# Hashed attention with adapters: a new order in the first head pair, adapter weight loads moved, and a finer split of weighted values

## The chip, the cores and the metric

The kernel runs on 1 core of one Trainium2 chip. The metric is the device time of one execution in microseconds (us), here the median of 5 executions. One more execution was recorded by the hardware profiler; it gives the profile page and the trace.

The engines have short names: PE is TensorE (matrix multiply; PEld is its weight load), ACT is ScalarE, DVE is VectorE, POOL is GpSimd, SP is SyncE, which only issues transfers.

## The reference, cut to what matters

Attention over 4 x 8 heads of 768 rows with 64 features. Each query and key gets a hash of 6 sign bits, and a query sees only the keys with its own hash. Then comes a mixture of 8 adapters of rank 16, two of them chosen per row.

```python
q_bits = (einsum('bhsd,dk->bhsk', q, proj) > 0)        # k_bits likewise, 6 bits
mask = q_bucket[:, :, :, None] == k_bucket[:, :, None, :]
scores = where(mask, (q @ k.T) / sqrt(D), -1e9)
attn = softmax(scores); x = attn @ v                    # x: [3072, 512]
logits = x @ w_gate; top two of 8, softmax over the two
out = x + sum over the two of w * ((x @ A[e]) @ B[e])
```

## The kernel before, in words

The 32 heads are worked in 16 pairs, p = 0 to 15. For a pair, queries and keys are transposed on PE (`trans`, line 232: three groups of four 128x128 transposes, each copied out of PSUM at line 249 by DVE or at line 247 by ACT into `qkT`). `hash` (line 256) multiplies `qkT` with the projection (line 262) and DVE turns the result into +-0.5 (`sgn`, line 265). Four small DMAs on SP (`sign_dma`, line 167; two from `hash`, two from `hash_b`) carry these rows into partitions 64 to 69 of the tile `aug`, which has the features in partitions 0 to 63 (`cast`, line 276, on POOL). Scores are taken over 71 rows of `aug`, so that the hash decides inside the same matmul.

The scores of a pair are made in 9 tiles of 128x1024 (`score`, line 320), one in each slot s = 0 to 8: two or three matmuls at line 327, then one exponential on ACT at line 329. There are two score buffers, so the matmuls of a tile wait for the exponential two tiles before. `pvmm(p, h, i0, i1)` (line 338) multiplies the exponentials of head h with the values `vb`, six matmuls at line 334 for each of six row groups i. `uniform` (line 358) makes a small term for rows without a match, `norm` (line 368) adds it on DVE, divides and writes `x`; after the second head POOL casts `x` into `xb`. `vcast` (line 218) prepares the values on POOL.

The order of work on every engine is written out by hand: the loop in `run` calls, in each slot, `score`, then `first_pair` (p = 0) or `pair` (p = 1 to 14) and `moe_slot`; `last_pair` does the last one. Each engine takes its instructions in that order, and what one needs from another is a wait on a semaphore. Pair p prepares pair p + 1 (last transposes in slot 0, casts in slot 1, hash in slot 2) and starts the transposes of pair p + 2 in slots 5 and 7. PSUM has eight banks: two score buffers of two banks each (`ps_s`), one bank T (`ps_t`), two banks V (`ps_v`) and one bank M (`ps_m`). Transposes and hashes go to T unless another bank is named.

In the first pair the kernel has nothing prepared. The prologue brings pair 0 far enough for its first score tiles; the hashes of the second head of pair 0 (`signs1`, line 155) and everything of pair 1 are done between the score tiles of pair 0, in `first_pair` (line 606).

The adapter weights are loaded on POOL's DMA queue by `load_moe(i)` (line 171): i = 0 the gate, 1 to 4 one slice of `A` each, 5 `B`. Gate and `A` go into the tile `wa`, first read in pair 5; `B` goes into `Bcat`, first read in slot 6 of pair 5. The adapters of a batch of four pairs are computed in the pairs of the next one, in groups of row slots given by `moe_group`: one or two slots for the first batches, three for batch 2 (pairs 13 and 14). `moe_slot` (line 571) does this: logits in slots 0 and 1 (line 480), the choice of experts (lines 489 to 513), a transpose in slot 4 (line 534), and `delta` from slot 6 on (line 548 on PE, line 556 on DVE).

Of the kernel before, what the change touches and what calls it, by code (L numbers as in the profile page):

```python
# [19 lines left out]
class Emitter:  # L20
# [585 lines left out]
    def first_pair(self, s):  # L606
        T, M, V = (self.ps_t, "t"), (self.ps_m, "m"), (self.ps_v, "v")
        if s == 0:
            self.load_qk(2)
            self.load_v(1)  # L610
            self.load_v(2)
        if s == 1:
            self.signs1(3, (T, M))
            self.trans(1, 0, bank=V)
        if s == 2:
            self.signs1(2, (T, M))
        if s == 3:
            self.trans(1, 1, on_act=True, bank=V)
            self.trans(1, 2)
            self.cast(1, 0)  # L620
            self.cast(1, 1)
        if s == 4:
            self.hash(1)
            self.hash_b(1)
        if s == 5:
            self.trans(2, 0, bank=M)
            self.vcast(1)
            self.load(3)
        if s == 6:
            self.pvmm(0, 0, 0, 2)  # L630
            self.uniform(0)
        if s == 7:
            self.pvmm(0, 0, 2, 4)
            self.trans(2, 1, bank=M)
        if s == 8:
            self.pvmm(0, 0, 4, 6)
            self.load_moe(0)
            self.load_moe(1)

    def pair(self, p, s):  # L640
        n = len(self.moe_group(p)[1])

        for at, i0, i1 in ((1, 0, 1), (3, 1, 3), (4, 3, 5), (5, 5, 6)) if n == 2 else ((1, 0, 2), (3, 2, 4), (4, 4, 6)):
            if s == at:
                self.pvmm(p - 1, 1, i0, i1)
        if s == 0:
            self.norm(p - 1, 0)
            self.trans(p + 1, 2)
            self.load_qk(p + 3, (0,))
        if s == 1:  # L650
            self.cast(p + 1, 0)
            self.cast(p + 1, 1)
        if s == 2:
            self.hash(p + 1)
            if p + 1 == self.n_pairs - 1:
                self.hash_b(p + 1)
            self.load_qk(p + 3, (1,))
        if s == 4:
            self.uniform(p)
            if p + 1 < self.n_pairs - 1:  # L660
                self.hash_b(p + 1)
        if s == 5:
            self.norm(p - 1, 1)
            self.vcast(p + 1)
            self.trans(p + 2, 0, on_act=n > 1)
            if p < 4:
                self.load_moe(p + 1)
            if p == 3:
                self.load_moe(5)
        if s == 6:  # L670
            self.pvmm(p, 0, 0, 2)
        if s == 7:
            if p % self.PPB:
                self.xturn(p - 1)
            self.trans(p + 2, 1)
            self.pvmm(p, 0, 2, 3)
        if s == 8:
            self.pvmm(p, 0, 3, 6)
            if p % self.PPB == 0:
                self.xtrans(p - 1, bank=(self.ps_m, "m"))  # L680
            self.load_v(p + 3)

    def last_pair(self, p, b):
        t = [(0, 1), (2, 3), (4, 5)]
# [101 lines left out]
```

## Time and profile before

| | us |
|---|---|
| median of 5 executions | 174.6 (173.92 to 175.15) |
| the profiled execution's own time | 174.27 |
| its span, first to last instruction | 172.5 |
| mean granted PE clock | 0.982 |
| score matmuls, line 327, x408 | 86.1 busy |
| value matmuls, line 334, x1080 | 48.1 busy |
| transposes, line 242, x180 | 27.9 busy |
| copies out of PSUM, line 249, x39 | 26.7 busy, 685 ns each |
| casts, line 280, x30 | 43.9 busy, 1463 ns each |

Matmuls overlap, so their busy time is longer than the time they hold the queue; the distance from one start to the next is the better measure. The exponentials follow each other at 0.90 to 0.92 us where nothing holds them up. The first exponential of a pair begins at these times, so that the distance is a pair's length:

| pair | first exponential, us | length, us |
|---|---|---|
| 0 | 8.54 | 10.69 |
| 1 | 19.23 | 9.22 |
| 2 | 28.45 | 8.86 |
| 3 | 37.31 | 8.86 |
| 13 | 130.70 | 10.61 |
| 14 | 141.31 | 9.87 |
| 15 | 151.18 | |

DMA issues on SP from the end of pair 0 are in this order: four sign transfers of pair 1 (15.43 to 18.86), the loads of pair 3 and half of those of pair 4 (18.96 to 20.88), two sign transfers of pair 2 (22.33), and so on. The transfers of the gate and of the first piece of `A` are issued on POOL at 19.86 and 20.77.

### The profile page before, as it was taken

To read this page: it belongs to the slowest core of one execution; us is meant where nothing else is said; L and a number is where in the kernel's file an instruction comes from. 1 tells how busy PE (TensorE), PEld (TensorE's weight loads), DVE (VectorE), ACT (ScalarE), POOL (GpSimd) and SP (SyncE) were. 2 spreads that over 40 slices of the span, in tenths; PEclk is the share of its full clock that TensorE was granted. 3 is DMA by queue.
4 is the path that set the end of the run, shared out by engine and by line. 5 is a ranking of instruction groups with operands and counts; after the bars stand their busy time and mean duration, and the time that the engine had idled before them with its cause. 6 is when DMAs were issued, how large, how long until landed. Compare 5 with 4: busy or idle time off the path is not lost.

```text
span 172.5 us, 5262 instructions
## 1 busy us (share of the span) xinstructions
PE 162.0 (94%) x2109; PEld 112.1 (65%) x2109; DVE 117.6 (68%) x315; ACT 151.1 (88%) x177; POOL 115.5 (67%) x140
## 2 busy tenths in 40 slices
PE   7999999999999999999999999999999999998850
PEld 5445667676757576767667676767687766687600
DVE  4865666564746787778687787868785776647770
ACT  3688998999998999999998999999998988997750
POOL 8289989597988657576756677686766566630280
PEclk9999999999999999999999999999999999999975
DMA  5990399769997139577876258586944024240036
GB/s 171 283 351 22 121 264 226 122 146 187 131 237 244 43 117 281 159 183 262 122 263 189 77 150 301 130 242 209 230 137 151 10 48 184 57 184 4 2 144 222
DMA packets 30402, 28.49 MB, mean 165 GB/s; under 512 B 15066, under 2 KB 28458, under 8 KB 30378
## 3 DMA queue, kind: packets, MB, share of 16 engines
q1 hardware_dynamic: 24984, 27.36, 54.6%
q0 software_dynamic: 4832, 0.27, 4.7%
q10 hardware_dynamic: 562, 0.53, 0.9%
q8 instruction: 16, 0.26, 0.6%
q14 instruction: 8, 0.07, 0.1%
HBM read 19.42 MB, written 6.29 MB: 149 GB/s over the span
## 4 chain that ended last, share of the span: by engine, by line
PE 78%; DVE 8%; DMA 4%; POOL 3%; issue 2%; ACT 1%; SPq 1%; DVEq 0%; ACTq 0%; POOLq 0%
PE s L327 31%; PE pv L334 16%; PE tr L242 12%; PE hs L262 7%; PE lz L480 3%; DMA aug<-sgn 3%; PE dl L548 2%; PE hsd L146 2%; DMA nat<-in_k_dram 2%; DVE qkT L249 2%; PE xtp L463 1%; DVE acc L556 1%; PE trf L125 1%; DVE x L384 1%; POOL xb L390 1%
## 5 line engine op out<-in xcount | busy, mean ns | idle before, releaser
L329 ACT ACTIVATE P<-s 128x1024 bf16<-128x1024 f32 x144 | 139.7, 1028 | 9.1 <-PE s L327 7.5
L327 PE MATMUL s<-aug 71*128 71x256 bf16 (+2 forms) x408 | 86.1, 316 | 0.6 <-ACT P L329 0.3
L334 PEld LDWEIGHTS <-P 128*128 128x128 bf16 x1080 | 45.4, 98 | 11.8
L280 POOL CAST aug<-qkT 64x1536 bf16<-64x1536 f32 x30 | 43.9, 1463 | 11.9 <-DVE qkT L249 9.6
L334 PE MATMUL pv<-vb,P 128*128 128x65 bf16 x1080 | 48.1, 193 | 0.0
L327 PEld LDWEIGHTS <-aug 71*128 71x128 bf16 x408 | 32.6, 97 | 19.1 <-issue 11.1
L249 DVE TENSOR_SCALAR qkT<-tr 128x512 f32<-128x512 f32 x39 | 26.7, 685 | 7.9 <-PE tr L242 6.0
L390 POOL CAST xb<-x 128x768 bf16<-128x768 f32 x15 | 12.3, 822 | 25.3 <-DVE x L384 23.2
L242 PE MATMUL tr<-ident,nat 128*128 128x128 f32 x180 | 27.9, 278 | 0.0
L242 PEld LDWEIGHTS tr<-ident,nat 128*128 128x128 f32 x180 | 20.3, 140 | 7.5 <-DVE qkT L249 3.1
L265 DVE TENSOR_SCALAR sgn<-hs 128x384 bf16<-128x384 f32 x15 | 8.4, 557 | 13.3 <-PE hs L262 11.9
L384 DVE TENSOR_TENSOR x<-pv,ri 128x384 f32<-128x384 f32 x30 | 16.7, 557 | 1.0
L556 DVE SCALAR_TENSOR_TENSOR acc<-dl,rt,x 128x512 f32<-128x512 f32 (+1 forms) x21 | 14.9, 719 | 3.3 <-PE dl L548 3.3
L379 DVE TENSOR_TENSOR pv<-pv,uni 128x390 f32<-128x390 f32 x24 | 13.6, 568 | 3.4 <-PE pv L334 3.3
L225 POOL TENSOR_TENSOR vs<-vn 128x384 f32<-128x384 f32 x16 | 15.9, 993 | 0.0
L262 PE MATMUL hs<-qkT,proj 128*32 128x384 f32 x120 | 12.8, 498 | 0.6 <-DVE qkT L249 0.3
L223 POOL CAST vb<-vn 128x768 bf16<-128x768 f32 x16 | 13.2, 825 | 0.1
L554 POOL TENSOR_TENSOR acc<-tmp,x 128x512 f32<-128x512 f32 x4 | 5.0, 1264 | 8.8 <-ACT tmp L553 8.8
L548 PE MATMUL dl<-Bcat,zmT 128*128 128x512 bf16 x24 | 9.5, 397 | 0.9 <-ACT zmT L537 0.8
L480 PE MATMUL lz<-wa,xT 128*128 128x136 bf16 x96 | 9.3, 223 | 0.6 <-ACT xT L465 0.6
L366 DVE COPY uni<-un 128x130 f32<-128x130 f32 x12 | 3.5, 294 | 6.8 <-PE un L364 6.8
L228 POOL TENSOR_TENSOR vb<-vs,vs 128x128 bf16<-128x128 f32 x16 | 7.3, 458 | 1.3
(70 smaller groups left out, 126.0 us busy)
## 6 DMA issues: line engine op xcount, KB each, us to landing
vn<-in_v_dram SPq DMA_DIRECT2D x16, 384.0 KB
nat<-in_q_dram SPq DMA_DIRECT2D x15, 384.0 KB
nat<-in_k_dram SPq DMA_DIRECT2D x15, 384.0 KB
out_dram<-acc SPq DMA_DIRECT2D x4, 512.0 KB
out_dram<-acc SPq DMA_DIRECT2D x8, 256.0 KB
out_dram<-acc SPq DMA_DIRECT2D x2, 768.0 KB
aug<-sgn SPq DMA_DIRECT2D x60, 9.0 KB
nat<-in_q_dram SPq DMA_DIRECT2D x2, 192.0 KB
```

The lines of the kernel that those rows point to most:

```text
L225: nc.gpsimd.tensor_add(out=s3, in0=vn[:, :, 0:3, :], in1=vn[:, :, 3:6, :])
L242: nc.tensor.transpose(out=ps[:, j * P:(j + 1) * P], in_=self.nat[p][:, idx % 2, idx // 2, u * P:(u + 1) * P], identity=self.ident)
L249: nc.vector.tensor_scalar(out=out, in0=ps, scalar1=2.0 ** -5, scalar2=None, op0=ALU.mult)
L262: nc.tensor.matmul(out=ps[32 * j:32 * j + 32, :], lhsT=self.proj2, rhs=self.qkT[p][:, j * 384:(j + 1) * 384], start=True, stop=True)
L280: self.nc.gpsimd.tensor_copy(out=self.aug[p % 2][0:64, :, e * n:(e + 1) * n], in_=self.qkT[p][64 * e:64 * e + 64, :].rearrange("p (j c) -> ...
L327: nc.tensor.matmul(out=ps[:, o:o + n], lhsT=aug[0:71, 2 * h + 1, kt * P:(kt + 1) * P], rhs=q, start=True, stop=True)
L329: nc.scalar.activation(out=self.P_[p][:, s * 1024:(s + 1) * 1024], in_=ps, func=ACT.Exp, scale=128.0)
L334: self.nc.tensor.matmul(out=pv, lhsT=self.p_at(p, h, kt, i), rhs=self.vb[p % 3][:, h, self.slot(kt), :], start=(start and kt == 0), stop=( ...
L384: nc.vector.tensor_tensor(out=self.x[b][:, :, c:c + D].rearrange("p (u e) d -> p e u d", e=2), in0=pv[:, 0:T, 0:D].rearrange("p (e u) d -> ...
L390: nc.gpsimd.tensor_copy(out=self.xb[b][:, hp], in_=self.x[b][:, :, hp * P:(hp + 1) * P])
L480: nc.tensor.matmul(out=lz[:, i, :], lhsT=self.xT[b][:, t, s * P:(s + 1) * P], rhs=self.wa[:, t, :], start=(t == 0), stop=(t == self.nD - 1))
L556: nc.vector.scalar_tensor_tensor(out=acc[:, i, c], in0=ps[:, c], scalar=self.rt[b, slots][:, i:i + 1], in1=self.x[b][:, slots[i], c], op0= ...
```

## The change

In the first pair the transposes of pair 1 begin one slot later and use other banks, and the second hash of slot 2 uses both V banks. The hash of pair 1 moves from slot 4 to slot 5, behind the sixth score tile, with its sign transfers and, behind them, the loads of pair 3. The first two transposes of pair 2 move from slots 5 and 7 to slots 7 and 8, and `uniform` uses bank M. The gate load moves from pair 0, slot 8, to pair 2, slot 8, and the load of `B` from pair 3, slot 5, to pair 4, slot 2. The values of the second head, which pairs with two adapter slots split over slots 1, 3, 4 and 5 as 1 + 2 + 2 + 1 row groups, are now split so with three adapter slots too (pairs 13 and 14), where they were 2 + 2 + 2 over slots 1, 3 and 4.

```diff
--- before.py
+++ after.py
@@ -611,36 +611,34 @@
             self.load_v(2)
         if s == 1:
             self.signs1(3, (T, M))
-            self.trans(1, 0, bank=V)
         if s == 2:
-            self.signs1(2, (T, M))
+            self.signs1(2, (V, V))
+            self.trans(1, 0)
         if s == 3:
-            self.trans(1, 1, on_act=True, bank=V)
-            self.trans(1, 2)
+            self.trans(1, 1, on_act=True, bank=M)
+            self.trans(1, 2, bank=V)
             self.cast(1, 0)
             self.cast(1, 1)
-        if s == 4:
+        if s == 5:
             self.hash(1)
             self.hash_b(1)
-        if s == 5:
-            self.trans(2, 0, bank=M)
+            self.load(3)
             self.vcast(1)
-            self.load(3)
         if s == 6:
             self.pvmm(0, 0, 0, 2)
-            self.uniform(0)
+            self.uniform(0, bank=M)
         if s == 7:
             self.pvmm(0, 0, 2, 4)
-            self.trans(2, 1, bank=M)
+            self.trans(2, 0)
         if s == 8:
             self.pvmm(0, 0, 4, 6)
-            self.load_moe(0)
+            self.trans(2, 1, bank=M)
             self.load_moe(1)
 
     def pair(self, p, s):
         n = len(self.moe_group(p)[1])
 
-        for at, i0, i1 in ((1, 0, 1), (3, 1, 3), (4, 3, 5), (5, 5, 6)) if n == 2 else ((1, 0, 2), (3, 2, 4), (4, 4, 6)):
+        for at, i0, i1 in ((1, 0, 1), (3, 1, 3), (4, 3, 5), (5, 5, 6)) if n > 1 else ((1, 0, 2), (3, 2, 4), (4, 4, 6)):
             if s == at:
                 self.pvmm(p - 1, 1, i0, i1)
         if s == 0:
@@ -655,6 +653,8 @@
             if p + 1 == self.n_pairs - 1:
                 self.hash_b(p + 1)
             self.load_qk(p + 3, (1,))
+            if p == self.PPB:
+                self.load_moe(5)
         if s == 4:
             self.uniform(p)
             if p + 1 < self.n_pairs - 1:
@@ -665,8 +665,6 @@
             self.trans(p + 2, 0, on_act=n > 1)
             if p < 4:
                 self.load_moe(p + 1)
-            if p == 3:
-                self.load_moe(5)
         if s == 6:
             self.pvmm(p, 0, 0, 2)
         if s == 7:
@@ -679,6 +677,8 @@
             if p % self.PPB == 0:
                 self.xtrans(p - 1, bank=(self.ps_m, "m"))
             self.load_v(p + 3)
+            if p == 2:
+                self.load_moe(0)
 
     def last_pair(self, p, b):
         t = [(0, 1), (2, 3), (4, 5)]
```

In the order of the instructions, the number of instructions of each engine is the same in both kernels.

## The prediction

> **What bounds the kernel now.** I write (p, s) for score tile s (0 to 8) of pair p. The page comes first: two engines are nearly full, and the exponentials alone fill 139.7 us, 1028 ns each.
>
> ```profile
> PE 162.0 (94%) x2109; PEld 112.1 (65%) x2109; DVE 117.6 (68%) x315; ACT 151.1 (88%) x177; POOL 115.5 (67%) x140
> q0 software_dynamic: 4832, 0.27, 4.7%
> L329 ACT ACTIVATE P<-s 128x1024 bf16<-128x1024 f32 x144 | 139.7, 1028 | 9.1 <-PE s L327 7.5
> ```
>
> ScalarE is idle only 9.1 us before exponentials, 7.5 of them for TensorE. So a microsecond is won only where both the exponentials and TensorE's queue come forward. The second line is the adapter weights: tiny packets, but 4.7% of 16 engines. Next, the chain of waits from 7 to 38 us (start, length, what):
>
> ```profile
> 13.13 0.70 DVE qkT L249
> 13.87 0.85 PE hs L262 x8
> 14.72 0.54 PE s L327 x3
> ...
> 20.34 0.55 PE s L327 x3
> 20.89 0.83 PE hs L262 x8
> 21.74 0.57 DVE sgn L265
> 22.33 0.75 SPq L168
> ...
> 23.13 4.53 DMA aug<-sgn
> 27.66 0.09 issue
> 27.75 0.59 PE s L327 x3
> ```
>
> Two things are to be seen. In pair 0 the hash of pair 1 stops TensorE's queue at 13.87 until VectorE has copied the transposes. At the end of pair 1, tile (2,0) starts at 27.75, right after the sign rows of pair 2 landed at 27.66, 4.53 us after the issue. The timeline puts the 18 weighted-value matmuls before it at 26.84 to 27.36 (start of the last), so TensorE was free at about 27.42: 0.33 us lost. The view of stretches shows why that landing was late (pair 1, pair 2; the last two figures are DMA share and GB/s):
>
> ```profile
> 18.49:27.75 9.26, 9.06 (x122) 6.07 (x119) 5.53 (x13) 8.98 (x10) 8.49 (x10) 1.00 1.02 229
> 27.75:36.70 8.95, 8.95 (x118) 6.10 (x119) 5.13 (x11) 8.29 (x10) 6.99 (x9) 1.00 0.83 161
> ```
>
> In pair 1 the DMA engines are full. Then the timeline of VectorE around the step from pair 0 to pair 1:
>
> ```profile
> 17.87 0.69 DVE L249 TENSOR_SCALAR qkT<-tr 128x512 f32<-128x512 f32 x1 [0.98 <-PE tr L242]
> ...
> 18.67 0.57 DVE L379 TENSOR_TENSOR pv<-pv,uni 128x390 f32<-128x390 f32 x1
> ...
> 19.51 0.56 DVE L384 TENSOR_TENSOR x<-pv,ri 128x384 f32<-128x384 f32 x1
> ...
> 19.98 0.68 DVE L249 TENSOR_SCALAR qkT<-tr 128x512 f32<-128x512 f32 x1
> ```
>
> It ends at 20.66, and the hash of pair 2 starts at 20.82. Last, TensorE in pair 14:
>
> ```profile
> 145.42 0.60 PE L327 MATMUL s<-aug 71*128 71x512 bf16 x2
> 145.86 0.53 PE L334 MATMUL pv<-vb,P 128*128 128x65 bf16 x12
> 146.35 0.34 PE L534 MATMUL ztp<-ident_bf,zm 128*128 128x128 bf16 x3
> 146.53 1.31 PE L327 MATMUL s<-aug 71*128 71x256 bf16 x6
> ```
>
> Twelve value matmuls take 0.37 us of queue, six take 0.19.
>
> **What the Trainium skill says.** "TensorE: Matmul & The Clock Gate", Part 3, The mechanism: matmuls are "strict FIFO, no reordering". The trace agrees: (0,5) needs nothing from the hash, and starts only behind it, at 14.66. "PSUM — Partial Sum Buffer", Engine vs sequencer instructions: ScalarE, VectorE and GpSimdE queues are strict FIFO; a copy put ahead of the norm delays the norm. "DMA: Bandwidth & Descriptors", Issuing engines are not separate DMA queues: whatever engine issues them, transfers share the same 16 engines and interleave; the 1.02 above agrees. The same page, Specifications, wants 512 B or more per transfer for line rate: here 4832 small packets took 4.7% x 172.5 x 16 / 4832 = 27 ns each.
>
> **Part 1, the first pair.** Nothing is added or removed; order and PSUM banks change. I replay it with the measured starts.
> - (0,2) now stands directly behind the hash of slot 1 (second pass at 9.20, next matmul 0.41 later) instead of behind four transposes (9.61 to 10.10). It waits for exponential 0 (8.54 + 1.02 = 9.57): about 9.65 for 10.10. Its exponential is then bound by ScalarE, 9.46 + 0.92 = 10.38 for 10.74.
> - The hash of slot 2 uses the two V banks, free since 8.82. It and then the transposes run behind (0,2): 1.25 us to the first transpose (0.22 + 0.30 + 0.32 + 0.41, the starts seen before), 0.49 to (0,3): 11.39 for 11.60. Eight transposes as before (0.45 + 0.87): (0,4) at 12.71 for 12.92, its exponential at 13.44 for 13.65.
> - (0,5) now has no hash in front: 13.15 for 14.66. Its exponential follows at 13.44 + 0.92 = 14.36 for 15.30. Here the first pair is 0.94 us ahead.
> - The hash of pair 1 waits for the copy of the last transposes: PE end 12.88, copy 12.94 to 13.63, hash 13.68 for 13.87. So although it stands one tile later, it runs 0.19 us earlier. Exponentials 6 and 7 follow at 15.27 and 16.17 (before 16.22, 17.12). GpSimd gains nothing: its two casts start behind line 114 at 14.02 as before.
> - The sign rows come 0.19 us earlier. Completion marks in the trace put the second of them at 18.40 now, against the start of (1,0) at 18.49. TensorE would be ready for (1,0) at 17.97, and waits until about 18.30. No bulk load lies in front of these rows on SP, whose order keeps the signs ahead of the loads.
> - The transposes of pair 2 move from slots 5 and 7 to 7 and 8. The second group is now at 17.54 (0,8 at 16.72, values 17.16), behind the values instead of before tile 8 at 17.20. Its copy starts at 18.21 for 17.87. VectorE goes in order: add 18.81, reciprocal 19.42, x 19.65, last copy 20.12 to 20.81. So the hash of pair 2 starts at 20.86, before 20.82.
>
> So the 0.94 us of lead is first cut to 0.2-0.3 by the sign rows and then to nothing (-0.04) by VectorE. This is the step that I trust least: at best, with the lead kept whole, 0.95 is won; at worst 0.2 us is lost.
>
> **Part 2, the adapter weights.** The gate weights (512 runs of 8 numbers: 128 partitions x 4) leave pair 0's slot 8 for pair 2's. At 27 ns they cost 512 x 27 / 16 = 0.86 us of all engines, an estimate; one A piece with 1024 runs costs 1.7. In pair 1 the rows of pair 2 wait behind four loads and both adapter pieces. Without the gate, and with loads issued 0.19 earlier, they land about 0.9 us earlier, near 26.7, before TensorE's 27.46. The 0.33 us wait goes, minus the 0.04: 0.29 won. If only a third of that relief comes, half of the gain remains. GpSimd's issue (0.91 us) goes from 19.86 as well; its casts then end at 23.75 for 24.66, needed only at 27.46, so worth nothing. In pair 2's slot 8 the gate goes in front of the casts of pair 4 (38.91 to 41.91 now) and pushes them to about 42.8. Behind them stands xb at 43.29, which waits 1.38 us for VectorE and covers it. The transfer may delay the sign rows of pair 4, which landed at 43.22; (4,0) needs them at about 45.5, so 0.86 fits. If the cover is gone, as in pair 1, at most 0.3 us is lost. The move of Bcat (0.56 us of GpSimd) from pair 3 to pair 4 is covered in the same way: xb at 52.16 has 0.84 us of idle before it, and Bcat is needed at pair 5's slot 6.
>
> **Part 3, pairs 13 and 14 (three adapter slots).** Six value matmuls move from slot 1 to 3, six from 3 to 4, six from 4 to 5. Everything between comes 0.19 us earlier. In pair 13 this is given back: slot 5's transposes start where they did, 136.23, and tile 8 and the wait of the last delta for VectorE (140.40) stay. In pair 14 no transposes follow. Tiles 2 to 5 start 0.19 earlier (146.34 for 146.53), tile 6 waits for exponential 4, itself earlier (147.06 for 147.25), and the deltas follow. The norm comes 0.19 later on VectorE (x 147.42 for 147.23) but ends at 147.97, just as the delta needs VectorE. Worth 0.19 us, between 0 and 0.25. The cast of the last values on GpSimd ends at 151.73 for 151.54, needed at 152.9.
>
> **Sum.** 0.29 + 0.19 = 0.48 us. After pair 2 all stages are relative to TensorE's queue, so it is carried to the end. The profiled execution took 174.27 us (span 172.5): 173.79. The median is 174.6: **174.1 us**.
>
> **Rivals.**
> - Lead kept (B): the wait at the sign rows and VectorE's chain are shorter than I reckon, as ScalarE is 0.95 us ahead at tile 7. 0.95 + 0.33 + 0.19 = 1.47 us: 173.1. For it: the lead up to tile 7 is plain. Against: rows at 18.2, and strict order on VectorE.
> - Rows late anyway (C): the wait at 27.66 comes from the loads, not from the gate weights. Then 0.15 to 0.2 us: 174.4.
> - Slower (D): the hash now stands behind (0,5), and if its rows take 4.53 us, as in pair 1, instead of about 2, the second lands at 16.31 + 4.53 = 20.84 and (1,0) starts at 20.93. The hash of pair 2 then follows 2.15 us later, 23.08 for 20.82: 2.3 us lost, 0.5 won back, 176.4. It decides from a landing past 19.1. Against: no load is under way from 14.5 to 19.
> - The change does what it says in all three parts, by the order of instructions; that is no rival.
>
> **Numbers.** A 50%, B 25%, C 12%, D 13%. This kernel can tell about 0.5%, 0.87 us, from no change. Faster: B nearly whole and a quarter of A, where small terms add up (0.24 + 0.13). Slower: D. The rest is the same. Range 173.0 to 175.0: it takes in B and C and leaves out D and B's lower edge.
>
> **What would show it.** Right: (0,5) at about 13.2; (1,0) at 18.2-18.4 beside the landing; the hash of pair 2 at 20.8-20.9; no DMA wait before (2,0); pair 14 shorter by 0.19 and pair 13 not. Wrong: a hash of pair 2 at 20.0 (B), a chain that still holds 4 us of sign rows in pair 1 (C), (1,0) past 19.1 (D).

## The result and the profile after

| | before | after |
|---|---|---|
| median, us | 174.43 (45 executions, 173.67 to 175.4) | 173.74 (26 executions, 173.26 to 174.64) |
| profiled execution, its span | 174.27, 172.5 | 173.32, 171.5 |

The ratio after to before is 0.9962, with a 95% interval of 0.9947 to 0.9976: 0.66 us won, with 0.42 to 0.92 us possible. The prediction said 0.48 us and 174.1 us.

The head of the page of after, in the order engines, adapter queue, chain by engine, exponentials:

```profile
PE 161.3 (94%) x2109; PEld 112.0 (65%) x2109; DVE 117.7 (69%) x315; ACT 151.2 (88%) x177; POOL 115.6 (67%) x140
...
q0 software_dynamic: 4832, 0.27, 4.9%
...
PE 82%; DVE 9%; POOL 3%; issue 2%; ACT 0%; DVEq 0%; ACTq 0%; POOLq 0%
...
L329 ACT ACTIVATE P<-s 128x1024 bf16<-128x1024 f32 x144 | 139.6, 1028 | 8.7 <-PE s L327 7.0
```

No engine does less work: the busy times are those of before within 0.7 us. What is gone is waiting. ScalarE's idle time for TensorE is 7.0 us (7.5 before), and no DMA stands in the third line any more. On the page of before that line was

```profile
PE 78%; DVE 8%; DMA 4%; POOL 3%; issue 2%; ACT 1%; SPq 1%; DVEq 0%; ACTq 0%; POOLq 0%
```

The first exponential does not start at the same moment in every execution: 8.54 us in the trace of before, 7.89 in that of after, and 7.92 to 9.10 in the experiments, where the prologue was not touched. So I compare lengths, and give all other times counted from the first exponential ("rel"). A pair's length is the distance of its first exponential from the next pair's.

| pair | before, us | after, us |
|---|---|---|
| 0 | 10.68 | 10.37 |
| 1 | 9.22 | 9.28 |
| 2 to 12, together | 102.26 | 102.26 |
| 13 | 10.60 | 10.64 |
| 14 | 9.87 | 9.68 |
| 0 to 14, together | 142.63 | 142.23 |

In the traces 0.25 us come from pairs 0 and 1 and 0.15 from pairs 13 and 14. The chain of waits of after, from 7 to 38 us, shows what sets the step from pair 1 to pair 2 (start, length, what):

```profile
17.00 0.48 PE tr L242 x4
17.49 0.02 issue
17.51 0.70 DVE qkT L249
18.21 0.02 issue
18.23 0.58 DVE pv L379
...
19.07 0.56 DVE x L384
19.63 0.61 DVE qkT L249
20.24 0.04 issue
20.28 0.85 PE hs L262 x8
...
26.47 0.55 PE pv L334 x18
27.01 0.44 PE s L327 x3
```

VectorE's copy, add, multiply and second copy stand nose to tail and release the hash of pair 2. Behind it the chain is all TensorE's: tile (2,0) follows the values directly, where before 4.53 us of sign rows and a stop stood. The view of stretches has the DMA share of pairs 1 and 2, each from its first score matmul to that of the next (the last two figures are that share and GB/s):

```profile
17.63:26.85 9.22, 8.87 (x117) 5.98 (x118) 5.87 (x12) 7.96 (x10) 7.59 (x9) 1.00 0.89 224
26.85:35.80 8.95, 8.95 (x124) 6.10 (x121) 5.29 (x11) 8.65 (x10) 7.35 (x9) 1.00 0.76 166
```

It was 1.02 in pair 1. 1.02 of 9.26 us is 9.4 us of all engines, 0.89 of 9.22 is 8.2: 1.2 us less. This can't be put down to the gate weights alone: in the two traces below with part 1 undone, the gate is gone from pair 1 too, and the figure is 10.1 and 9.4 us. It adds up the times of the packets that begin in the stretch, so it can pass 1 and is a rough measure. The gate's own 512 packets, added up in the trace of before, took 11.7 us of one engine, 0.73 us of all 16; 0.86 was reckoned. Last, TensorE in pair 14:

```profile
144.80 0.53 PE L334 MATMUL pv<-vb,P 128*128 128x65 bf16 x12
145.29 0.34 PE L534 MATMUL ztp<-ident_bf,zm 128*128 128x128 bf16 x3
145.47 0.60 PE L327 MATMUL s<-aug 71*128 71x256 bf16 x3
145.91 0.35 PE L334 MATMUL pv<-vb,P 128*128 128x65 bf16 x6
146.19 0.59 PE L327 MATMUL s<-aug 71*128 71x512 bf16 x3
```

Six of the value matmuls now stand between two score tiles that were back to back before.

### The profile page after: what moved, and what is told of

Same layout as the page of the kernel before. It is cut to its first block, busy times and chain, and to the rows that moved or that the text cites. A ratio compares the mean times of both kernels' runs of the same rounds, so it can differ in the third digit from the quotient of the medians.

```text
span 171.5 us, 5263 instructions
## 1 busy us (share of the span) xinstructions
PE 161.3 (94%) x2109; PEld 112.0 (65%) x2109; DVE 117.7 (69%) x315; ACT 151.2 (88%) x177; POOL 115.6 (67%) x140
## 4 chain that ended last, share of the span: by engine, by line
PE 82%; DVE 9%; POOL 3%; issue 2%; ACT 0%; DVEq 0%; ACTq 0%; POOLq 0%
PE s L327 33%; PE pv L334 17%; PE tr L242 12%; PE hs L262 7%; PE lz L480 3%; PE dl L548 3%; DVE qkT L249 2%; PE hsd L146 2%; PE warm L188 1%; DVE x L384 1%; PE xtp L463 1%; DVE acc L556 1%; PE ztp L534 1%; PE trf L125 1%; POOL xb L390 1%
## 5 line engine op out<-in xcount | busy, mean ns | idle before, releaser
L327 PEld LDWEIGHTS <-aug 71*128 71x128 bf16 x408 | 32.7, 97 | 18.9 <-issue 10.8
```

The source lines that it names most:

```text
L327: nc.tensor.matmul(out=ps[:, o:o + n], lhsT=aug[0:71, 2 * h + 1, kt * P:(kt + 1) * P], rhs=q, start=True, stop=True)
```

## The experiments

The runs of before taken beside them had medians of 174.03 us (first three), 174.28 (next four) and 174.33 (last four). The ratios are not quotients of the medians printed here and differ from them by up to 0.0014, some 0.25 us; so small differences between times say little. "0+1" is pairs 0 and 1 together. The theory was that the gate weights make the rows of pair 2 late, and that VectorE's chain eats the first pair's lead; the rivals were that the lead, or the loads alone, decide.

### Each part taken back

**Part 1 undone** (order and banks of the first pair as before, parts 2 and 3 kept), from after to the experiment, shortened:

```diff
-        if s == 5:
+        if s == 4:
             self.hash(1)
             self.hash_b(1)
-            self.load(3)
+        if s == 5:
+            self.trans(2, 0, bank=M)
             self.vcast(1)
+            self.load(3)
...
-            self.trans(2, 0)
+            self.trans(2, 1, bank=M)
```

> Part 1 undone: the first pair of the kernel before, with the moved adapter loads and the finer values. Distances between the first exponentials of pairs; before: pair 0 10.69, pair 1 9.22, pair 14 9.87; changed kernel: 10.37, 9.28, 9.68. My theory (the new first pair gives its lead back, the gain there is the missing gate load): pair 0 stays at 10.69, pair 1 falls to about 8.9, their sum 19.55 to 19.6, no worse than the changed kernel's 19.65; pair 14 at 9.68; time 0.5 us under before, ratio 0.997. Rival, the new first pair is what gains: the sum stays at about 19.9, ratio 0.999.

Then one more execution of the same kernel, with its trace:

> Part 1 undone once more, for a second execution's trace. If the slowest DMA engine scatters between executions, the wait before (2,0), 0.65 us in the first trace, is smaller here: pair 1 between 8.9 and 9.4. If the old first pair makes the rows late by itself, pair 1 is 9.5 again.

Measured: 173.86 us, ratio 0.9976 (0.9959 to 0.9993); the second execution took 174.44 us. Pair 0 is 10.69 us in both traces, so the first pair's order is worth 0.32 there. But pair 1 takes 9.54 and 9.60 us, not 8.9: the wait before (2,0) is still there, though the gate weights are gone. TensorE's timeline in the second trace:

```profile
26.72 0.71 PE L334 MATMUL pv<-vb,P 128*128 128x65 bf16 x18
28.01 0.59 PE L327 MATMUL s<-aug 71*128 71x512 bf16 x3 [0.59 <-DMA aug<-sgn]
```

**Part 2 undone** (gate and `B` loaded where they were):

```diff
+            self.load_moe(0)
             self.load_moe(1)
...
-            if p == self.PPB:
-                self.load_moe(5)
...
+            if p == 3:
+                self.load_moe(5)
...
-            if p == 2:
-                self.load_moe(0)
```

> Part 2 undone: the gate weights are loaded in pair 0 again, B in pair 3; the rest as in the changed kernel. My theory: tile (2,0) waits again for the sign rows of pair 2, which land behind both adapter pieces; the loads start 0.2 earlier than before, so the wait is 0.05 to 0.3 us, and pairs 0 and 1 take 19.7 to 19.95 us together for 19.65. Rival, the loads of queries, keys and values make the rows late and not the gate: 19.65 unchanged.

> Part 2 undone once more, for a second execution's trace. My theory: with both adapter pieces beside the loads the rows of pair 2 come late in every execution, pair 1 9.4 or more. If the 0.42 us of the first trace were chance: pair 1 near 9.28.

Measured: 174.09 us, ratio 0.9993 (0.9972 to 1.0013): no gain is left to be seen. The second execution took 174.59 us. 0+1 is 20.09 and 20.14 us in the two traces (after 19.65), with 0.44 and 0.50 us of wait at the rows of pair 2.

The completion marks explain both. The second sign transfer of pair 2 (issued at 14.6 to 14.7 rel) has seven marks: one at once, then one for each of six DMA engines, of which the last decides. The Trainium skill, "DMA: Bandwidth & Descriptors", Why a DMA increments its semaphore by 16 and not by 1, says that a semaphore "climbs by 1 as each engine's data lands"; the traces agree, with six steps after the first.

| kernel, trace | fifth of six marks, rel | last mark, rel | TensorE ready, rel | wait |
|---|---|---|---|---|
| before | 18.71 | 19.12 | 18.85 | 0.36 |
| after | 17.96 | 18.00 | 18.96 | none |
| part 3 undone | 17.61 | 17.95 | 18.95 | none |
| part 1 undone | 18.12 | 19.44 | 18.85 | 0.68 |
| part 1 undone, again | 18.36 | 19.50 | 18.85 | 0.74 |
| part 2 undone | 19.03 | 19.31 | 18.96 | 0.44 |
| part 2 undone, again | 19.13 | 19.36 | 18.95 | 0.50 |

(TensorE is ready 0.55 us after the start of its last 18 value matmuls, the step seen in after; the wait is counted from there to the start of (2,0), which comes some 0.09 us after the landing.) With the gate back, the last two of the six engines are late and the other four in time, in two traces of two. With the first pair's old order and no gate, five engines are in time and one is 1.1 to 1.3 us behind them, again in two of two. In before, too, it is one engine alone that comes after TensorE is ready. So the gate weights are a cause, but taking them away alone is not seen to help in a trace: only with the new order does the wait vanish, in both traces that have the two parts.

The times do not bear this last step out. By its traces, part 1 undone should be slower than before: pairs 0 to 14 take 142.80 and 142.91 us, for 142.63. Timed, it is faster, by 0.24% with 0.07 to 0.41% possible, and its interval overlaps that of after. So a wait as long as in these two traces can't be the rule in its executions, and what the gate is worth with the old order stays open.

**Part 3 undone**:

```diff
-... if n > 1 else ((1, 0, 2), (3, 2, 4), (4, 4, 6)):
+... if n == 2 else ((1, 0, 2), (3, 2, 4), (4, 4, 6)):
```

> Part 3 undone: with three adapter slots the values are split 2 + 2 + 2 again. My theory: pair 14 back to 9.87 from 9.68, pair 13 unchanged at 10.61 to 10.64, all else as in the changed kernel; 0.19 us more, a ratio 0.001 above the changed kernel's. Rival, the finer split is worth nothing or acts in pair 13 too: pair 14 at 9.68, or pair 13 longer than 10.64.

Measured: 173.76 us, ratio 0.9985 (0.9961 to 1.0009), too wide for 0.2 us. The trace is sharp: pair 14 takes 9.91 us (after 9.68), pair 13 10.61 (after 10.64), and pairs 0 to 12 are those of after within 0.01. Part 3 is worth 0.20 us in the trace. Over all traces pair 14 is 9.68 to 9.73 us with the finer split and 9.87 to 9.91 with the old one.

### What holds the lead of the first pair

**Transposes of pair 2 one slot earlier**, so that VectorE copies them before it needs to normalise:

```diff
             self.uniform(0, bank=M)
+            self.trans(2, 0)
         if s == 7:
             self.pvmm(0, 0, 2, 4)
-            self.trans(2, 0)
+            self.trans(2, 1, bank=M)
         if s == 8:
             self.pvmm(0, 0, 4, 6)
-            self.trans(2, 1, bank=M)
             self.load_moe(1)
```

> The changed kernel with the first two transpose groups of pair 2 one slot earlier each (slots 6 and 7 for 7 and 8). My theory: VectorE's order (copy, norm, copy) eats the lead of pair 0 before the hash of pair 2; with the copy out of the way that hash starts about 0.4 us earlier, at 12.0 after the first exponential for 12.39, and pairs 0 and 1 together take about 19.25 for 19.65; ratio to before about 0.994. Rival, the landing of the sign rows of pair 1 alone sets the pace: no change, 19.65.

Measured: 173.91 us, ratio 0.9984 (0.9963 to 1.0005). In the trace the hash of pair 2 comes at 11.97 rel for 12.39, and 0+1 is 19.36 us for 19.65. The times do not show these 0.29 us: the ratio expected was 0.994, outside the interval, and after's own is 0.9962. The trace's chain of waits:

```profile
17.61 0.37 PE pv L334 x12
17.97 0.25 issue
18.22 0.59 PE s L327 x3
...
20.06 0.47 PE s L327 x3
20.52 0.78 PE hs L262 x8
```

VectorE has left the chain. What is left in front of (1,0) is a stop of 0.25 us, and the second sign transfer of pair 1 landed at 18.13. So the sign rows and then VectorE's chain limit the lead, in the order that the prediction gave them. In this trace (2,0) waits again for the rows of pair 2, 0.13 us: TensorE comes 0.42 us earlier and the last of the six engines late.

**Second sign transfer of pair 1 issued from ScalarE**, beside SP's first:

```diff
-            self.sign_dma(nc.sync, p, j, sgn)
+            self.sign_dma(nc.scalar if p == 1 and j == 1 else nc.sync, p, j, sgn)
```

> The changed kernel with the second sign transfer of pair 1 issued on ScalarE beside SP's first. My theory: the rows land 0.7 to 1.0 us earlier, tile (1,0) starts 0.2 to 0.3 earlier (9.45 after the first exponential for 9.74), but the hash of pair 2 stays at 12.39 because VectorE's chain ends then; pairs 0 and 1 together 19.65, no gain; ratio as the changed kernel. Rival, the rows set the pace: hash and sum 0.3 earlier.

Measured: 174.65 us, ratio 1.0029 (1.0012 to 1.0045): slower. The chain of waits shows a part of the reason:

```profile
15.04 0.62 ACTq L168
15.66 0.05 issue
15.71 1.03 ACT P L329
16.74 0.04 issue
16.79 0.59 PE s L327 x3
...
21.02 0.85 PE hs L262 x8
```

The rows do land earlier: the two transfers, issued together, are in at 16.86 and 17.22, the last at 9.11 rel against 9.65 in after. But the transfer waits on ScalarE's queue for `sgn`, its issue takes 0.62 us, and the exponential behind it starts at 15.71 instead of 14.80. Tile 8, the transposes and VectorE's chain follow, and the hash of pair 2 comes at 12.91 rel, 0.52 later than in after.

That makes 0+1 0.53 us longer than in after, but pairs 0 to 14 are only 0.13 longer than in before (142.76 us). The rest lies behind the last exponential: from its end to the end of the span it is 11.87 us here and 11.95 in the next kernel, against 11.38 to 11.49 in ten of the other eleven traces and 11.70 in one. With ScalarE's transfer SP waits for eight semaphores at the close instead of seven; that this is the cause is not shown.

**Both together**, the last two edits in one kernel:

> Both: early transposes of pair 2 and the second sign transfer of pair 1 on ScalarE. My theory: each removes one of two waits in series behind the same lead, so the gains add: hash of pair 2 at about 11.65 to 11.75 for 12.39, pairs 0 and 1 together 18.9 to 19.05; ratio to before about 0.992 to 0.993. Rival, one wait alone counts: no better than the better of the two alone.

Measured: 173.87 us, ratio 0.9968 (0.995 to 0.9986); 0+1 is 19.25 us, not 18.9 to 19.05: the gains did not add. The hash of pair 2 comes at 11.98 rel, as with the early transposes alone. The rows are in at 9.06 rel, but exponential 7, the one two tiles before (1,0), is late behind the transfer's issue and ends at 9.50; (1,0) starts at 9.75, as in after. What is left of the gain against 19.36 us is at the rows of pair 2, which (2,0) does not wait for here.

**Loads of pair 3 ahead of the sign rows of pair 1**, the rival that was to make it slower, brought about by an edit:

```diff
         if s == 5:
+            self.load(3)
             self.hash(1)
             self.hash_b(1)
-            self.load(3)
```

> The changed kernel with the loads of pair 3 issued in front of the sign rows of pair 1 on SP. The slower rival of my prediction at work: rows behind 1.15 MB of loads land 1 to 3 us later, tile (1,0) starts at 10.8 to 12.7 after the first exponential for 9.74, and pairs 0 and 1 together grow by 0.7 to 2.5 us. If rows are not held up by loads in the same queue: 19.65 unchanged.

One execution: 174.01 us. The chain of waits:

```profile
15.60 2.84 DMA aug<-sgn
18.44 0.09 issue
18.53 0.59 PE s L327 x3
...
20.37 0.47 PE s L327 x3
20.83 0.78 PE hs L262 x8
```

The rows take 2.84 us, and (1,0) starts 0.82 us later than in after (10.56 rel for 9.74). Of this only 0.40 reaches the hash of pair 2 (12.79 rel), since VectorE would have held it until 12.39 anyway; 0+1 is 20.05 us, 0.40 more than after, and less than the 0.7 to 2.5 expected.

### A better place for the query load

**Before, with the queries of pair 4 loaded behind the sign rows of pair 2** (all three parts of the change undone):

```diff
             self.trans(p + 1, 2)
-            self.load_qk(p + 3, (0,))
+            if p > 1:
+                self.load_qk(p + 3, (0,))
...
-            self.load_qk(p + 3, (1,))
+            self.load_qk(p + 3, (1,) if p > 1 else (0, 1))
```

> The kernel before with one thing changed: in pair 1 the query load of pair 4 is issued behind the first two sign transfers of pair 2 and not in front of them. My theory: the wait of tile (2,0) for these rows is the whole of what pair 1 of the kernel before loses against 8.86; the rows then land at least 0.7 us earlier and pair 1 falls from 9.22 to 8.86 to 8.95, ratio 0.998. Rival, pair 1 is long for another reason (the first pair's late norm on VectorE): pair 1 stays at 9.2.

Measured: 173.86 us, ratio 0.9981 (0.996 to 1.0001). The rows of pair 2 land at 18.20 rel, five engines at 17.04 (before 19.12 and 18.71), and (2,0) waits no more. But pair 1 is 9.15 us, not 8.9, for another transfer was late:

```profile
18.78 5.23 DMA nat<-in_k_dram
24.01 0.04 issue
24.05 0.33 PE tr L242
```

This is the key load of pair 3. All its engines but one were done at 22.64; the last came at 24.01, and TensorE lost 0.30 us before the transposes.

**After, with the early transposes and this late query load**, the two edits above in one kernel:

> The changed kernel with the early transposes of pair 2 and with the query load of pair 4 behind the sign rows of pair 2. My theory: both remaining losses go, hash of pair 2 at 11.97 after the first exponential, no DMA wait before (2,0), pairs 0 and 1 together 19.25 to 19.3 in any execution; ratio to before 0.994 to 0.996. Rival: the order of loads shifts the wait to a later tile, which needs rows or queries that now come later, and pair 2 grows beyond 8.86.

Measured: 173.26 us (172.9 to 174.12) against 174.33, ratio 0.9941 (0.9922 to 0.996). 0+1 is 19.23 us, pairs 0 to 14 are 141.82 us (after 142.23), and the rows of pair 2 are in at 17.03 rel, 1.5 us before TensorE wants them. The page's lines of the chain by engine and of the exponentials:

```profile
PE 83%; DVE 7%; POOL 3%; issue 2%; ACT 1%; POOLq 1%; ACTq 0%; DVEq 0%
...
L329 ACT ACTIVATE P<-s 128x1024 bf16<-128x1024 f32 x144 | 139.8, 1028 | 8.2 <-PE s L327 6.4
```

Pair 2 stays at 8.86 us, so no later tile takes over the wait. ScalarE's idle time for TensorE falls from 7.0 to 6.4 us (6.5 with the early transposes alone). This version beats before clearly. Against after its advantage is 0.41 us in the traces; the two intervals against before overlap slightly, and the two were not timed side by side.

## Why the prediction was right, point by point

**Part 1, the replay of the first pair: right in its times.** Counted from the first exponential, predicted and measured starts are:

| start of | predicted, rel | after, rel |
|---|---|---|
| (0,2), (0,3), (0,4), (0,5) | 1.11, 2.85, 4.17, 4.61 | 1.08, 2.85, 4.16, 4.59 |
| hash of pair 1 | 5.14 | 5.12 |
| (1,0), behind the sign rows | 9.76 | 9.74 |
| VectorE's copy, add, x, last copy | 9.67, 10.27, 11.11, 11.58 | 9.62, 10.34, 11.18, 11.66 |
| hash of pair 2 | 12.32 | 12.39 |

The step trusted least, that the lead of 0.94 us is cut to nothing by the sign rows and by strict order on VectorE, held: the hash of pair 2 is even 0.11 us later than before (12.28 rel), where 0.04 was reckoned. The early transposes showed the cause: with VectorE out of the way 0.42 us comes back at this hash.

**Part 2, the rows of pair 2: right in the outcome, not shown to be the gate's alone.** Landing was put at 18.16 rel and came at 18.00; the wait vanished, and pairs 0 and 1 gained 0.25 us against 0.29. The wait was 0.36 us and not 0.33, and VectorE's part -0.11 and not -0.04, which together give the 0.25. Undoing part 2 brings the wait back. But the prediction had the gate's 0.86 us of DMA time (0.73 in the trace) do it, with 0.19 us from the earlier loads as a help. Taken away alone, the gate gave 0.35 to 0.6 us at the fifth mark and nothing at the last one, which came 0.3 to 0.4 us later than in before. Part 1 and part 2 are not independent terms of the sum, as it had them. Where the gate and `B` were moved to they cost nothing: pairs 2 to 12 take 102.26 us in both traces.

**Part 3: right.** Pair 14 gained 0.19 us in after and gives 0.23 back when part 3 is undone; pair 13 gave it all back, and a further 0.04.

**Sum.** 0.25 + 0.19 - 0.04 = 0.40 us in the two traces, against 0.48 predicted and 0.66 (0.42 to 0.92) timed. From pair 15 on, the trace of after is 0.10 us longer (21.42 for 21.32), so the two traces account for 0.30 us, less than the timed interval allows. They are one execution each; what the executions win beyond it is not located. That the forecast came so near is in part luck: landing in time rests on an engine that comes late in other traces, and the sum lies between what the traces and what the times give.

**Rivals.** The kept lead (B) lost at the two places named. "Rows late anyway" (C) is what the traces with part 1 undone show, not that of after. The slower rival (D) was priced wrongly: I gave the delay of (1,0) in full to the hash of pair 2, and the rows 4.53 us. Behind the loads they took 2.84 us, and VectorE's chain left 0.4 us of slack, so that 0.40 us was lost, not 2.3. The mechanism is real; its price term was too large.

## What to carry to other kernels

When an early stage gains a lead, replay each queue up to the next meeting point: a strict-order engine that merely moves an unhurried copy in front of an urgent one can use up the whole lead. A transfer spread over several DMA engines is as late as its slowest one, so read the marks of the engines one by one before a late landing is put down to the bytes in front. Moving a bulk load that isn't needed yet behind small urgent transfers on the same issuing queue brought these in 0.9 us earlier in one kernel here and 1.6 us in another (18.58 to 17.03 rel).

## What the runs showed of the hardware

- **One late engine.** In four of the traces (part 1 undone twice, the early transposes, before with the late query load) one DMA engine ended a sign transfer 0.8 to 1.3 us behind the other five; in after and with the loads first it did not. In before it was 0.4 us. The trace doesn't name the engine of a mark. One candidate is the queue that the page calls instruction, on the page of after

```profile
q8 instruction: 16, 0.26, 0.7%
```

with 16 packets of 16 KB, each on one engine for 0.7% x 171.5 x 16 / 16 = 1.2 us on average. In the two traces with part 1 undone one of them ran from 18.42 to 19.36 and from 18.16 to 19.15 rel, and the last marks came at 19.44 and 19.50. With the early transposes one ran from 17.14 to 18.35, and the last mark came at 18.58. But in before with the late query load the next such packet began at 18.84, after the late mark at 18.20, and in after one ran from 16.60 to 18.24 with no engine late. The cause stays open.
- **A DMA issue on a computing engine.** On ScalarE it kept the exponential behind it back by 0.9 us (0.62 us of issue and the wait for `sgn`), for a landing 0.54 us earlier.
- **The start scatters.** The first exponential began between 7.89 and 9.10 us in the thirteen traces, with the same prologue. Spans of single traces can't be compared below 1 us; lengths between exponentials repeat within 0.05 us where no DMA decides.
